# The last stage of an attention and two-MLP kernel: products of the result placed between the products of a and b

## The chip, the cores and the metric

The kernel runs on one core of a Trainium2 chip. Times are device microseconds of one execution; the kernel before takes 856.04 us as a median of 3 runs (854.52 to 856.62), lower is better. TensorE is called PE here, VectorE DVE, ScalarE ACT, GpSimd POOL, and SyncE, which issues DMAs, SP.

## The reference

Attention (a pooled one and a banded one, added) makes x of 2304 x 512. Two MLPs follow, and the change lies in the second:

```python
def _moe_ref(x, w_in, w_out):          # d_ff 2048
    h = x @ w_in
    g = h * np.cos(h)
    return (g @ w_out).astype(np.float32)

def _moe2_ref(x, w1, w2, w3, w_out):   # d_model 512, d_ff 1024
    a = x @ w1
    b = x @ w2
    h = a * b @ w3
    return (h @ w_out).astype(np.float32)
```

## The kernel before

The kernel is recorded by a small planner. Each piece of work is a generator (`Job`, lines 191 to 202) with an urgency; it asks for an engine, a buffer or a condition. `run` (264) gives an engine that its own cost estimates call free to the most urgent job whose inputs they call visible. The result is one fixed order of instructions for each engine; on the chip every engine takes its queue in that order and waits at the head of it for what is missing. All instructions are recorded in one helper, so all have line 131 in the profile, and one goes by tile names.

The second MLP is stage 2, the last 280 us. w3 @ w_out was multiplied beforehand into one matrix (`w5`), so the result is (a * b) @ w5. The 2304 tokens are taken in 3 blocks j of 768, d_ff in 8 slices f of 128, which makes 24 steps n = 8 j + f (`steps2`). In a step, PE makes 7 products `ps_ab` (128 x 384, `ab_job`, 993): a recombination scheme of Strassen's kind, in which 7 products of quarter matrices replace the 8 that a and b would need. Numbers are split into a high and a low part, so a product of PE is 3 matmuls for each half of the contraction, 6 in all (`mm3`, 401). `sums_job` (955) recombines the 7 products: ACT copies product 0 to SBUF, DVE then makes seven additions that read products 1 to 6, product 4 twice. These tiles are called `v`. Product 1 gives a0, half of a; the additions of product 5 and 6 complete b0 and a1. `m_half_job` (944) multiplies a and b for each half of the 768 tokens on POOL (`v<-v`), casts the high part on ACT (`m<-v`) and subtracts for the low part on POOL (`m<-v,m`). Six products `ps_o` (128 x 512, 3 matmuls each, `o_job`, 1020) then add the step's share of the result: o0 to o2 need half 0 of m, o3 to o5 half 1.

Two PSUM banks are left for `ps_ab`. They are used in turn, so product k + 2 waits until product k has been read by ACT or DVE. The other six banks hold `ps_o`, which accumulates over the 8 steps of a block; at the end of a block ACT and DVE copy the six tiles out (`o_out_job`, 1040).

`y_in_job` loads the next block's x as `yr` and makes the seven right-hand operands `y` of the 7 products: sums of quarters (`yr<-yr`, DVE) and, for each, a cast on ACT (`y<-yr`) and two subtractions on POOL or DVE (`y<-yr,y`). Buffers for these come free one by one while the last step of a block (n = 7 and n = 15) uses the old ones. `w5_back_job` splits a slice of w5 for each step (`w<-w5r` on ACT, `w<-w5r,w` on DVE).

Before the change the products of the result are a job of their own with urgency base + 1000.5, behind `ab_job` with base + 1000. PE takes an o product only when the planner holds that the next `ps_ab` can't start. Line 1001 keeps the two together: step n may begin when step n - 2 of the result is done.

Of the kernel before, what the change touches and what calls it, by code (L numbers as in the profile page):

```python
# [21 lines left out]
P = 128  # L22
# [5 lines left out]
F2 = DFF2 // P  # L28
# [14 lines left out]
N2 = 768  # L43
NH = N2 // 2
NCH2 = NT // N2
NQ = 7
# [12 lines left out]
OUT_BANKS = (4, 5, 6, 7, 2, 3)  # L59
# [11 lines left out]
def fused_kernel(ctx: ExitStack, tc: tile.TileContext, qk_block, v_block, qk_pool, v_pool,  # L71
# [63 lines left out]
    ve, se, pe, ge, sy = (Engine(*e) for e in (("ve", nc.vector), ("se", nc.scalar), ("pe", nc.tensor), ("ge", nc.gpsimd), ("sy", nc.sync)))  # L135
# [29 lines left out]
    done = {}  # L165
# [17 lines left out]
    def bank(n, name):  # L183

        return psum.tile([P, 512], F32, name=name, tag=f"bank{n}", bufs=1)
# [18 lines left out]
    def on(name, fn, *aps, when=lambda: True):  # L204
        yield name, fn, aps, when

    def until(cond):
        while not cond():
            yield "until", cond

    def at_hand(name):
        return sorted(x for x in free[name] if x[0] <= now[0])

    def take(name, n=1, spare=lambda: 0):

        yield from until(lambda: len(at_hand(name)) >= n + spare())
        got = at_hand(name)[:n]
        for x in got:
            free[name].remove(x)
        return got[0][1] if n == 1 else [x[1] for x in got]  # L220
# [15 lines left out]
    def give(name, slot, engine):  # L236
        free[name].append((ends[engine] + LATENCY[engine], slot))
# [5 lines left out]
    def count(key, n=1):  # L243
        done[key] = done.get(key, 0) + n
# [60 lines left out]
    w_t = {}  # L305
# [89 lines left out]
    def mm3(out_ap, st, mv, first, last):  # L395

        (sh, sl), (mh, ml) = st, mv
        pe.matmul(out_ap, lhsT=sh, rhs=ml, start=first, stop=False)
        pe.matmul(out_ap, lhsT=sl, rhs=mh, start=False, stop=False)
        pe.matmul(out_ap, lhsT=sh, rhs=mh, start=False, stop=last)  # L400
# [487 lines left out]
    ys, ms = {}, {}  # L888
    steps2 = [(j, f) for j in range(NCH2) for f in range(F2)]
# [45 lines left out]
    def value():  # L935
        yield from until(lambda: any(len(at_hand(name)) > keep for name, keep in VALUES))
        name = next(name for name, keep in VALUES if len(at_hand(name)) > keep)
        slot = yield from take(name)
        return buf(slot, "v", [NH]), slot

    def give_value(slot, engine):
        give(slot[0], slot, engine)
# [12 lines left out]
    def sums_job(n, base, ps):  # L955

        def product(k):
            yield from until(lambda: k in ps)
            return ps[k]

        def plus(x, k, last=True):
            at, p = ps[k]
            z, slot = yield from value()
            yield from on("ve", lambda: ve.tensor_tensor(out=z, in0=x, in1=p, op=ALU.add), x, p)
            if last:
                give("bank", at, "ve")
            return z, slot

        at, p = yield from product(0)
        p1, p1_slot = yield from value()  # L970
        yield from on("se", lambda: se.copy(p1, p), p)
        give("bank", at, "se")
        yield from product(1)
        a0, a0_slot = yield from plus(p1, 1)
        yield from product(2)
        u, u_slot = yield from plus(p1, 2)
        give_value(p1_slot, "ve")
        yield from product(3)
        v, v_slot = yield from plus(u, 3)
        yield from product(4)  # L980
        w, w_slot = yield from plus(u, 4, False)
        give_value(u_slot, "ve")
        b1, b1_slot = yield from plus(v, 4)
        yield from product(5)
        b0, b0_slot = yield from plus(v, 5)
        give_value(v_slot, "ve")
        Job(base + n, m_half_job(n, 0, a0, b0, a0_slot, b0_slot))
        yield from product(6)
        a1, a1_slot = yield from plus(w, 6)
        give_value(w_slot, "ve")  # L990
        Job(base + n, m_half_job(n, 1, a1, b1, a1_slot, b1_slot))

    def ab_job(base):
        yield from until(reached("h", NSTEPS))
        got = []
        while not {2, 3} <= set(got):
            got.append((yield from take("bank")))
        for at in got:
            give("bank" if at < 2 else f"bank{at}", at if at < 2 else 0, "pe")
        for n, (j, f) in enumerate(steps2):  # L1000
            yield from until(lambda: j in ys and done.get("o", 0) >= n - 1)
            ps = {}
            Job(base + n - 0.5, sums_job(n, base, ps))
            for k in range(NQ):
                q = NQ * f + k
                yield from until(lambda: k in ys[j] and ("w12", q // 2) in w_t)
                at = yield from take("bank")
                p = bank(at, "ps_ab")[:, :NH]
                w, (y, y_slot) = w_t["w12", q // 2][0][:, q % 2], ys[j][k]
                yield from on("pe", lambda: [mm3(p, (w[:, 0, c * P:(c + 1) * P], w[:, 1, c * P:(c + 1) * P]), (y[:, 0, c], y[:, 1, c]), c == 0, c == 1) for c in range(2)], y, w)  # L1010
                ps[k] = at, p
                if f == F2 - 1:
                    give("x", y_slot, "pe")
                if j == NCH2 - 1 and (q % 2 or q == NQ * F2 - 1):
                    give("w", w_t["w12", q // 2][1], "pe")
            if f == 0 and j + 1 < NCH2:
                Job(base + n + 4, y_in_job(j + 1))
            count("ab")

    def o_job(base):  # L1020
        for n, (j, f) in enumerate(steps2):
            if f == 0:
                ps = []
            for t in range(N2 // P):
                half, to = divmod(t, NH // P)
                yield from until(lambda: (n, half) in ms and ("w5", n) in w_t)
                (m, m_slot), (w, w_slot) = ms[n, half], w_t["w5", n]
                if f == 0:
                    yield from take(f"bank{OUT_BANKS[t]}")
                    ps.append(bank(OUT_BANKS[t], f"ps_o{t}"))  # L1030
                ts = slice(to * P, (to + 1) * P)
                yield from on("pe", lambda: mm3(ps[t], (m[:, 0, ts], m[:, 1, ts]), (w[:, 0, :], w[:, 1, :]), f == 0, f == F2 - 1), m, w)
                if f == F2 - 1:
                    Job(base + n - 2, o_out_job(j, t, ps[t]))
                if to == NH // P - 1:
                    give("g", m_slot, "pe")
            give("w", w_slot, "pe")
            count("o")

    def o_out_job(j, t, ps):  # L1040
        slot, name = (yield from take("t")), "ve" if t % 2 else "se"
# [15 lines left out]
    with tc.manual_schedule():  # L1057
# [76 lines left out]
        base = W5 + NSTEPS  # L1134
# [3 lines left out]
            Job(base + n - 6, w5_back_job(n))  # L1138
        Job(base - 8, y_in_job(0))
        Job(base + 1000, ab_job(base))  # L1140
        Job(base + 1000.5, o_job(base))
        run(reached("out", NT // P))


# [51 lines left out]
```

## Time and profile before

| | us |
|---|---|
| median of 3 runs | 856.04 (854.52 to 856.62) |
| profiled execution, device time | 858.45 |
| its span, first to last instruction | 856.7 |
| first `ps_ab` of stage 2 starts at | 575.04 |
| `ps_ab` in all, busy | 184.8 |
| `ps_o` in all, busy | 107.1 |

The profiled execution took 858.45 us, 2.4 us more than the median; its span is 856.7 us, and 1.75 us lie around it. In the timeline a row is a run of equal instructions: its start, how long it lasted, how many, and in brackets the time its engine stood idle before it and what ended that. Matmuls overlap, so a run's length contains about 0.16 us that the next run has begun in; starts are compared with starts. The chain of waits lists what led to the end, piece by piece, without such overlap.

### The profile page before, as it was taken

Reading aid. Unit: us, or ns where it says so; the run is one execution under the profiler, and the core shown is the slowest. Engines: PE = TensorE matmul, PEld = TensorE weight load, DVE = VectorE, ACT = ScalarE, POOL = GpSimd, SP = SyncE. Lnnn points to the kernel's source line nnn. Section 1 sums busy time; section 2 is a strip of 40 time slices with the busy share of each in tenths; the row PEclk is TensorE's granted clock in tenths of the full one; section 3 lists DMA queues with packets and bytes.
Section 4 is the critical chain, followed back from the end, with each engine's and each line's share of the span. In section 5 each row is a group of like instructions: output and inputs, shape, how many; then the busy total and the mean of one; then the engine's idle time right before and its main releaser. Section 6 shows DMA issues by size and latency. Waiting matters only on the chain.

```text
span 856.7 us, 14977 instructions
## 1 busy us (share of the span) xinstructions
PE 839.6 (98%) x5645; PEld 758.4 (89%) x5645; DVE 502.9 (59%) x897; ACT 446.6 (52%) x911; POOL 366.2 (43%) x330
## 2 busy tenths in 40 slices
PE   8999989999999999999999999999999999999998
PEld 7554579999999899998999999999999999999997
DVE  6988859975538783687446534625335633363442
ACT  2646689885767675677765756641112311241112
POOL 1013569855442345254533533524334633363322
PEclk9999999999999999999999999999999999999999
DMA  9989991131445532554255249681000500021011
GB/s 265 299 236 316 280 366 66 54 121 50 144 157 166 172 114 94 195 163 141 90 173 151 89 126 376 222 272 61 25 26 26 173 25 25 13 92 32 25 26 74
DMA packets 59625, 118.25 MB, mean 138 GB/s; under 512 B 18249, under 2 KB 25673, under 8 KB 59553
## 3 DMA queue, kind: packets, MB, share of 16 engines
q1 hardware_dynamic: 53040, 108.63, 39.7%
q10 hardware_dynamic: 6512, 8.67, 2.8%
q8 instruction: 44, 0.72, 0.4%
q14 instruction: 29, 0.23, 0.1%
HBM read 89.49 MB, written 27.79 MB: 137 GB/s over the span
## 4 chain that ended last, share of the span: by engine, by line
PE 83%; DVE 6%; DMA 5%; ACT 2%; issue 1%; ACTq 0%; POOL 0%; SPq 0%; DVEq 0%
PE ps_y L131 20%; PE ps_ab L131 20%; PE ps_h L131 19%; PE ps_o L131 12%; PE ps_w L131 5%; DVE t L131 2%; PE ps_av L131 2%; PE ps_tb L131 2%; DMA raw<-w3t 2%; DVE c L131 1%; PE ps_s L131 1%; DMA w_sc<-w 1%; PE ps_p L131 1%; DMA raw<-w_in 1%; PE ps_sb L131 1%
## 5 line engine op out<-in xcount | busy, mean ns | idle before, releaser
L131 PE MATMUL ps_y<-g,wo 128*128 128x384 f32 x1152 | 223.4, 338 | 0.4 <-POOL g L131 0.4
L131 PE MATMUL ps_h<-xs,wi 128*128 128x384 f32 x1152 | 219.5, 337 | 0.7 <-ACT ptp L131 0.5
L131 PEld LDWEIGHTS ps_y<-g,wo 128*128 128x128 f32 x1152 | 199.2, 188 | 4.6 <-issue 2.3
L131 PEld LDWEIGHTS ps_h<-xs,wi 128*128 128x128 f32 x1152 | 199.9, 188 | 3.5 <-issue 1.5
L131 PE MATMUL ps_ab<-y,w 128*128 128x384 f32 x1008 | 184.8, 336 | 0.9 <-DVE v L131 0.8
L131 PEld LDWEIGHTS ps_ab<-y,w 128*128 128x128 f32 x1008 | 176.8, 188 | 6.4 <-issue 1.4
L131 POOL TENSOR_TENSOR g<-c,g 128x384 fp32r<-128x384 f32 x96 | 106.5, 1109 | 157.1 <-ACT g L131 137.7
L131 DVE TENSOR_TENSOR v<-v,ps_ab 128x384 f32<-128x384 f32 x168 | 90.9, 553 | 139.8 <-ACT w L131 76.8
L131 ACT ACTIVATE c<-c 128x384 f32<-128x384 f32 x192 | 100.5, 524 | 36.2 <-DVE c L131 32.9
L131 POOL TENSOR_TENSOR v<-v 128x384 f32<-128x384 f32 x48 | 50.4, 1053 | 144.3 <-DVE v L131 142.5
L131 PE MATMUL ps_o<-w,m 128*128 128x512 f32 x432 | 107.1, 392 | 0.0
L131 DVE SCALAR_TENSOR_TENSOR c<-turns,ps_h 128x384 f32<-128x384 int32 x96 | 52.7, 549 | 79.2 <-ACT turns L131 71.5
L131 ACT CAST m<-v 128x384 fp32r<-128x384 f32 x48 | 24.5, 515 | 141.5 <-POOL v L131 141.5
L131 PEld LDWEIGHTS ps_o<-w,m 128*128 128x128 f32 x432 | 80.4, 188 | 14.1
L131 DVE SCALAR_TENSOR_TENSOR c<-c,ps_h 128x384 f32<-128x384 f32 x96 | 52.7, 549 | 55.8 <-ACT c L131 55.6
L131 ACT CAST g<-c 128x384 fp32r<-128x384 f32 x96 | 49.2, 512 | 41.5 <-DVE c L131 37.0
L131 ACT ACTIVATE turns<-ps_h 128x384 int32<-128x384 f32 x96 | 46.7, 487 | 37.2 <-PE ps_h L131 37.0
L131 PE MATMUL ps_w<-w,w 128*128 128x512 f32 x128 | 61.6, 608 | 1.5 <-DVE w L131 1.5
L131 ACT ACTIVATE t<-raw 128x512 f32<-128x512 f32 x72 | 47.8, 675 | 14.7 <-DMA raw<-w3t 5.9
L131 DVE TENSOR_SCALAR t<-t 128x512 int32<-128x512 int32 x72 | 46.7, 662 | 11.2 <-ACT t L131 11.2
L131 POOL TENSOR_TENSOR xs<-xb,xs 128x512 fp32r<-128x512 f32 (+1 forms) x24 | 27.1, 1129 | 51.0 <-ACT xs L131 47.3
L131 POOL TENSOR_TENSOR m<-v,m 128x384 fp32r<-128x384 f32 x48 | 47.8, 1017 | 0.0
(87 smaller groups left out, 862.5 us busy)
## 6 DMA issues: line engine op xcount, KB each, us to landing
w_sc<-w SPq DMA_DIRECT2D x56, 256.0 KB
w<-w_sc SPq DMA_DIRECT2D x28, 512.0 KB
raw<-w SPq DMA_DIRECT2D x24, 512.0 KB
raw<-w3t SPq DMA_DIRECT2D x16, 512.0 KB
raw<-w_in SPq DMA_DIRECT2D x16, 512.0 KB
raw<-w_out SPq DMA_DIRECT2D x16, 512.0 KB
w5r<-w_sc SPq DMA_DIRECT2D x24, 256.0 KB
kb<-qk_block SPq DMA_DIRECT2D x12, 408.0 KB
```

The lines of the kernel that those rows point to most:

```text
L131: return call(*args, **kw)
```

## The change

`o_job` is gone. `ab_job` itself issues the six products of the result of step n - 1 between the seven products of step n: one after product 2, 3, 4 and 5, two after product 6. A last round issues those of step 23 alone. The condition that step n - 2 of the result is done at the start of step n goes with it; the order now says it.

```diff
--- before.py
+++ after.py
@@ -997,45 +997,50 @@
             got.append((yield from take("bank")))
         for at in got:
             give("bank" if at < 2 else f"bank{at}", at if at < 2 else 0, "pe")
-        for n, (j, f) in enumerate(steps2):
-            yield from until(lambda: j in ys and done.get("o", 0) >= n - 1)
-            ps = {}
-            Job(base + n - 0.5, sums_job(n, base, ps))
+        ps_o = {}
+        for n in range(len(steps2) + 1):
+            if n < len(steps2):
+                j, f = steps2[n]
+                yield from until(lambda: j in ys)
+                ps = {}
+                Job(base + n - 0.5, sums_job(n, base, ps))
             for k in range(NQ):
-                q = NQ * f + k
-                yield from until(lambda: k in ys[j] and ("w12", q // 2) in w_t)
-                at = yield from take("bank")
-                p = bank(at, "ps_ab")[:, :NH]
-                w, (y, y_slot) = w_t["w12", q // 2][0][:, q % 2], ys[j][k]
-                yield from on("pe", lambda: [mm3(p, (w[:, 0, c * P:(c + 1) * P], w[:, 1, c * P:(c + 1) * P]), (y[:, 0, c], y[:, 1, c]), c == 0, c == 1) for c in range(2)], y, w)
-                ps[k] = at, p
-                if f == F2 - 1:
-                    give("x", y_slot, "pe")
-                if j == NCH2 - 1 and (q % 2 or q == NQ * F2 - 1):
-                    give("w", w_t["w12", q // 2][1], "pe")
-            if f == 0 and j + 1 < NCH2:
+                if n < len(steps2):
+                    q = NQ * f + k
+                    yield from until(lambda: k in ys[j] and ("w12", q // 2) in w_t)
+                    at = yield from take("bank")
+                    p = bank(at, "ps_ab")[:, :NH]
+                    w, (y, y_slot) = w_t["w12", q // 2][0][:, q % 2], ys[j][k]
+                    yield from on("pe", lambda: [mm3(p, (w[:, 0, c * P:(c + 1) * P], w[:, 1, c * P:(c + 1) * P]), (y[:, 0, c], y[:, 1, c]), c == 0, c == 1) for c in range(2)], y, w)
+                    ps[k] = at, p
+                    if f == F2 - 1:
+                        give("x", y_slot, "pe")
+                    if j == NCH2 - 1 and (q % 2 or q == NQ * F2 - 1):
+                        give("w", w_t["w12", q // 2][1], "pe")
+                if n:
+
+                    for t in {2: (0,), 3: (1,), 4: (2,), 5: (3,), 6: (4, 5)}.get(k, ()):
+                        yield from o_product(base, n - 1, t, ps_o)
+            if n < len(steps2) and f == 0 and j + 1 < NCH2:
                 Job(base + n + 4, y_in_job(j + 1))
-            count("ab")
-
-    def o_job(base):
-        for n, (j, f) in enumerate(steps2):
-            if f == 0:
-                ps = []
-            for t in range(N2 // P):
-                half, to = divmod(t, NH // P)
-                yield from until(lambda: (n, half) in ms and ("w5", n) in w_t)
-                (m, m_slot), (w, w_slot) = ms[n, half], w_t["w5", n]
-                if f == 0:
-                    yield from take(f"bank{OUT_BANKS[t]}")
-                    ps.append(bank(OUT_BANKS[t], f"ps_o{t}"))
-                ts = slice(to * P, (to + 1) * P)
-                yield from on("pe", lambda: mm3(ps[t], (m[:, 0, ts], m[:, 1, ts]), (w[:, 0, :], w[:, 1, :]), f == 0, f == F2 - 1), m, w)
-                if f == F2 - 1:
-                    Job(base + n - 2, o_out_job(j, t, ps[t]))
-                if to == NH // P - 1:
-                    give("g", m_slot, "pe")
-            give("w", w_slot, "pe")
-            count("o")
+            if n:
+                give("w", w_t["w5", n - 1][1], "pe")
+                count("o")
+
+    def o_product(base, n, t, ps):
+
+        (j, f), (half, to) = steps2[n], divmod(t, NH // P)
+        yield from until(lambda: (n, half) in ms and ("w5", n) in w_t)
+        (m, m_slot), (w, w_slot) = ms[n, half], w_t["w5", n]
+        if f == 0:
+            yield from take(f"bank{OUT_BANKS[t]}")
+            ps[t] = bank(OUT_BANKS[t], f"ps_o{t}")
+        ts = slice(to * P, (to + 1) * P)
+        yield from on("pe", lambda: mm3(ps[t], (m[:, 0, ts], m[:, 1, ts]), (w[:, 0, :], w[:, 1, :]), f == 0, f == F2 - 1), m, w)
+        if f == F2 - 1:
+            Job(base + n - 2, o_out_job(j, t, ps[t]))
+        if to == NH // P - 1:
+            give("g", m_slot, "pe")
 
     def o_out_job(j, t, ps):
         slot, name = (yield from take("t")), "ve" if t % 2 else "se"
@@ -1138,7 +1143,6 @@
             Job(base + n - 6, w5_back_job(n))
         Job(base - 8, y_in_job(0))
         Job(base + 1000, ab_job(base))
-        Job(base + 1000.5, o_job(base))
         run(reached("out", NT // P))
```

PE, the third step of stage 2, from its product 2 on; `y_...` are operands of a and b, `w_...` weights, `ps_o_...` the six banks of the result. Before:

```order
L131 MATMUL ps_ab<-y_6357,w_6236 128x384 x6
L131 MATMUL ps_ab<-y_6316,w_6236 128x384 x6
L131 MATMUL ps_ab<-y_6393,w_6259 128x384 x6
L131 MATMUL ps_ab<-y_6416,w_6259 128x384 x6
L131 MATMUL ps_o_6813<-w_6422,m 128x512 x3
L131 MATMUL ps_ab<-y_6643,w_6282 128x384 x6
L131 MATMUL ps_o_6859<-w_6422,m 128x512 x3
L131 MATMUL ps_o_6871<-w_6422,m 128x512 x3
L131 MATMUL ps_o_6878<-w_6422,m 128x512 x3
L131 MATMUL ps_o_6885<-w_6422,m 128x512 x3
L131 MATMUL ps_o_6892<-w_6422,m 128x512 x3
```

The same step on PE after the change:

```order
L131 MATMUL ps_ab<-y_6357,w_6236 128x384 x6
L131 MATMUL ps_o_6820<-w_6422,m 128x512 x3
L131 MATMUL ps_ab<-y_6316,w_6236 128x384 x6
L131 MATMUL ps_o_6835<-w_6422,m 128x512 x3
L131 MATMUL ps_ab<-y_6393,w_6259 128x384 x6
L131 MATMUL ps_o_6850<-w_6422,m 128x512 x3
L131 MATMUL ps_ab<-y_6416,w_6259 128x384 x6
L131 MATMUL ps_o_6864<-w_6422,m 128x512 x3
L131 MATMUL ps_ab<-y_6643,w_6282 128x384 x6
L131 MATMUL ps_o_6880<-w_6422,m 128x512 x3
L131 MATMUL ps_o_6888<-w_6422,m 128x512 x3
```

The work is the same; the two kinds alternate in five stretches each in place of two.

DVE, the last step of the first block (n = 7), from the last additions of step 6 on; `y_7397` and `y_7407` are operands 1 and 3 of the next block, `w_7381` is w5 of step 7, `yr` the quarters being subtracted. Before:

```order
L131 TENSOR_TENSOR v<-v,ps_ab 128x384 x5
L131 TENSOR_TENSOR y_7397<-yr,y_7397 128x384 x2
L131 TENSOR_TENSOR v<-v,ps_ab 128x384
L131 TENSOR_TENSOR y_7407<-yr,y_7407 128x384
L131 TENSOR_TENSOR w_7381<-w5r,w_7381 128x512
L131 TENSOR_TENSOR y_7407<-yr,y_7407 128x384
L131 TENSOR_TENSOR yr<-yr 128x2x384
L131 TENSOR_TENSOR v<-v,ps_ab 128x384
L131 TENSOR_TENSOR yr<-yr 128x2x384
```

The same place on DVE after the change, with the same tiles under other numbers (7396, 7411 and 7377):

```order
L131 TENSOR_TENSOR v<-v,ps_ab 128x384 x5
L131 TENSOR_TENSOR y_7396<-yr,y_7396 128x384 x2
L131 TENSOR_TENSOR w_7377<-w5r,w_7377 128x512
L131 TENSOR_TENSOR y_7411<-yr,y_7411 128x384 x2
L131 TENSOR_TENSOR yr<-yr 128x2x384
L131 TENSOR_TENSOR v<-v,ps_ab 128x384
L131 TENSOR_TENSOR yr<-yr 128x2x384
```

The addition of product 1 of step 7 (a0, the first single `v<-v,ps_ab` in either list) has moved behind four more operations: w, both halves of operand 3, and the first of the two large subtractions. The last step of the second block (n = 15) changes in the same way.

PE at the end of the program, from product 5 of step 23 on. Before:

```order
L131 MATMUL ps_ab<-y_8316,w_6683 128x384 x6
L131 MATMUL ps_o_8437<-w_8931,m 128x512 x3
L131 MATMUL ps_ab<-y_8339,w_6683 128x384 x6
L131 MATMUL ps_o_8496<-w_8931,m 128x512 x3
L131 MATMUL ps_o_8522<-w_8931,m 128x512 x3
L131 MATMUL ps_o_8527<-w_8931,m 128x512 x3
L131 MATMUL ps_o_8533<-w_8931,m 128x512 x3
L131 MATMUL ps_o_8540<-w_8931,m 128x512 x3
L131 MATMUL ps_o_8437<-w_9027,m 128x512 x3
```

After the change, from the same product:

```order
L131 MATMUL ps_ab<-y_8294,w_6683 128x384 x6
L131 MATMUL ps_o_8514<-w_8927,m 128x512 x3
L131 MATMUL ps_ab<-y_8312,w_6683 128x384 x6
L131 MATMUL ps_o_8527<-w_8927,m 128x512 x3
L131 MATMUL ps_o_8534<-w_8927,m 128x512 x3
L131 MATMUL ps_o_8470<-w_9023,m 128x512 x3
```

Between the last product of a and b and the first product of the last step's result stand two products of the result in place of five; the last row of each list is that first product (`w_9027`, `w_9023` are w5 of step 23).

## Rows read from the trace of the kernel before

**Rows 1.** The page's first part: busy time, share of the span, instructions.
```profile
PE 839.6 (98%) x5645; PEld 758.4 (89%) x5645; DVE 502.9 (59%) x897; ACT 446.6 (52%) x911; POOL 366.2 (43%) x330
```

**Rows 2.** Chain of waits, a regular step (start us, us, what; x counts matmuls).
```profile
640.26 6.27 PE ps_ab L131 x36
646.53 0.70 PE ps_o L131 x3
647.23 1.06 PE ps_ab L131 x6
648.29 3.44 PE ps_o L131 x15
```

**Rows 3.** Timeline of PE at the two changes of block.
```profile
651.57 2.27 PE L131 MATMUL ps_ab<-y,w 128*128 128x384 f32 x12
...
662.04 5.40 PE L131 MATMUL ps_ab<-y,w 128*128 128x384 f32 x30
667.86 2.34 PE L131 MATMUL ps_ab<-y,w 128*128 128x384 f32 x12 [0.41 <-DVE v L131]
670.04 0.86 PE L131 MATMUL ps_o<-w,m 128*128 128x512 f32 x3
...
760.41 2.35 PE L131 MATMUL ps_ab<-y,w 128*128 128x384 f32 x12 [0.41 <-DVE v L131]
```

**Rows 4.** Timeline of ACT in step 7, which starts at 651.57.
```profile
652.84 0.84 ACT L131 CAST y<-yr 128x768 fp32r<-128x768 f32 x1 [2.31 <-PE ps_ab L131]
653.58 0.47 ACT L131 COPY v<-ps_ab 128x384 f32<-128x384 f32 x1
...
654.68 0.62 ACT L131 CAST w<-w5r 128x512 fp32r<-128x512 f32 x1
```

**Rows 5.** Timeline of DVE in step 7 and just behind it.
```profile
653.71 1.03 DVE L131 TENSOR_TENSOR y<-yr,y 128x384 fp32r<-128x384 f32 x2 [4.82 <-ACT y L131]
654.65 0.55 DVE L131 TENSOR_TENSOR v<-v,ps_ab 128x384 f32<-128x384 f32 x1
...
655.58 0.69 DVE L131 TENSOR_TENSOR w<-w5r,w 128x512 fp32r<-128x512 f32 x1
...
656.77 0.96 DVE L131 TENSOR_TENSOR yr<-yr 128x768 f32<-128x768 f32 x1
657.65 0.55 DVE L131 TENSOR_TENSOR v<-v,ps_ab 128x384 f32<-128x384 f32 x1
...
663.77 1.84 DVE L131 TENSOR_TENSOR y<-yr,y 128x384 fp32r<-128x384 f32 x2
...
666.15 1.09 DVE L131 TENSOR_TENSOR w<-w5r,w 128x512 fp32r<-128x512 f32 x1
```

**Rows 6.** Timeline of PE and POOL at the end of the program.
```profile
843.00 0.86 PE L131 MATMUL ps_o<-w,m 128*128 128x512 f32 x3
...
844.76 7.68 PE L131 MATMUL ps_o<-w,m 128*128 128x512 f32 x33
...
846.56 1.99 POOL L131 TENSOR_TENSOR m<-v,m 128x384 fp32r<-128x384 f32 x2
```

**Rows 7.** Timeline of PE early in the program: its three longest waits.
```profile
15.38 1.71 PE L131 MATMUL ps_s<-qkd 64*72 64x144 f32 x8 [2.31 <-DVE qkd L131]
24.18 1.99 PE L131 MATMUL ps_w<-w,w 128*128 128x512 f32 x4 [1.55 <-DVE w L131]
115.78 0.71 PE L131 MATMUL ps_p<-ptp,vd 72*64 72x144 f32 x8 [1.77 <-DVE vd L131]
```

**Rows 8.** PE busy in stretches (bounds, length, busy, granted clock, DMA share, GB/s).
```profile
16.00:18.00 2.00, 2.00 (x10) 0.50 1.00 394
18.00:20.00 2.00, 2.00 (x14) 0.71 1.05 317
24.00:26.00 2.00, 1.82 (x4) 1.00 0.98 357
116.00:118.00 2.00, 2.00 (x17) 1.00 0.96 216
```

## The prediction

> **What bounds the kernel now.** I read the page's busy shares first: PE is busy 98% of the span and no other engine over 59% [rows 1]. So only what PE waits for, or does more slowly, can move the end. Next came the chain of waits over stage 2: from the first `ps_ab` to the last `ps_o` it is almost all PE, and in a regular step it shows four pieces without a gap [rows 2]. The timeline of PE then shows where PE does wait in this stage: once at each change of block, for an addition on DVE that frees a bank of `ps_ab` [rows 3]. Last, the timelines of ACT, DVE and POOL around the first of these places and around the end tell when the inputs come [rows 4 to 6].
>
> A model of PE's stage follows from rows 2. Six products of a and b in a row take 6.27, a single one 1.06: each further one costs (6.27 - 1.06) / 5 = 1.042, and an edge, where PE turns to them from the result, 1.06 - 1.042 = 0.018. Five products of the result take 3.44, one 0.70: each further one (3.44 - 0.70) / 4 = 0.685, and the edge 0.015. A pair of edges is 0.033, with the rounding of the rows 0.02 to 0.045. A regular step is 7 x 1.042 + 6 x 0.685 + 2 pairs = 11.47, as the four rows sum to.
>
> **Part 1, the finer alternation.** In each of 23 steps there are now 5 stretches of each kind, 115 pairs of edges in all; before there were 48 (two a step, one more at each change of block). 67 more pairs x 0.033 = +2.2. Bounds by rounding 1.3 to 3.0, and 0 if an edge is nothing but the profile's rounding.
>
> **Part 2, regular steps: no new wait.** Let R be the start of what stands behind product 5. At the end of the program R = 843.00, and the low part of half 0 is ready after the first of two subtractions, 846.56 + 1.99 / 2 = 847.55, that is R + 4.55; half 1 at R + 5.55 [rows 6]. The order of POOL and ACT in a regular step stays, and product 6 still stands one result product behind product 5, so these offsets hold. PE now comes to o0 after o3, product 6, o4 and o5, and products 0 to 2 of the next step: 0.70 + 1.06 + 1.385 + 3.15 = R + 6.3. That leaves 1.7 of slack; o3 comes 5.3 later still and needs half 1 only. If this cover were gone, each of 23 steps would pay what is missing. In the first step no result products stand between, so PE comes to o0 after only four products, 4.2 behind R, up to 0.4 early: +0.2 (0 to 0.4).
>
> **Part 3, the two changes of block: a long new wait.** Here the queue of DVE decides. In step 7 (start 651.57) product 3 needs the bank of product 1, which the addition a0 frees. Before, a0 ran at 654.65, right behind the two subtractions of operand 1 [rows 5]. Now w5's subtraction, both of operand 3 and the first large subtraction stand ahead of it. Walked through with these rows' durations:
> - ACT casts operand 1 at 652.84 and copies product 0 from 653.58 to 654.05 [rows 4]. Product 2 needs that bank; by the model PE is there at 651.57 + 2 x 1.042 + 0.018 = 653.67, and starts at 654.15. (0.1 from an engine's end to PE's start is an estimate; from the cast's end at 653.68 to DVE at 653.71 rows 4 and 5 show 0.03.) Before, a result product stood between and hid this.
> - DVE: operand 1 from 653.71 to 654.74; w, whose cast now comes before that of operand 3, to 655.34; operand 3, with its cast done at about 655.3, two subtractions of 0.5, to 656.38; the large subtraction, 0.96, to about 657.3; a0, 0.55, to 657.85 [rows 4, 5].
> - Product 3 can start at 657.95. Unhindered it would start at 651.57 + 3.15 + 0.70 = 655.42. Lost 2.53, and 0.08 for starting again: after the wait in rows 3 two products took 670.04 - 667.86 = 2.18 in place of 2.10. 2.6 in all.
>
> What is behind it: the additions of products 2 and 3 and the second large subtraction, which are done before PE needs their banks; the operands' casts and POOL's subtractions move later by as much as PE does. In step 8 PE's fixed order finds every bank free by the same walk. The same order stands at n = 15, so 2 x 2.6 = +5.2. Bounds from the nearest rows: nothing at all, if a0's place does not count; and if POOL works at the same time, the two pairs of operand subtractions cost 1.84 each in place of 1.03 and w 1.09 in place of 0.69 [rows 5], 2.0 more a change, +9.2. I take the uncontended rows, since POOL's last work on step 6, half 1, ends near 651.57 - 3.15 + 5.55 = 654.0.
>
> On this the Trainium skill (SBUF — State Buffer, Who interferes with whom) says that a DVE instruction with two SBUF inputs and a GpSimd instruction that reads SBUF can't share the port, and the loser blocks. Rows 5 agree (1.84 against 1.03); by that rule alone the sum would lie between +7.6 and +11.6, by when POOL works.
>
> The waits of before at the same places go. From 662.04 to 670.04 PE did seven products, 7 x 1.042 + 0.018 = 7.31, in 8.00 [rows 3]: 0.69 each, -1.4 together. What is late next there is part 3's own wait, a step earlier.
>
> **Part 4, the end.** Before, five products of the result covered the making of m of the last step, and 33 matmuls ran through from 844.76 [rows 6]. Now PE comes to the last step's o0 at R + 0.70 + 1.06 + 1.385 = R + 3.15, and half 0 is ready at R + 4.55: +1.4 (1.0, as the first of o0's three matmuls needs only the high part, to 1.7). Half 1 is there before o3, R + 5.55 against R + 6.6. The copies and DMAs behind are unchanged.
>
> **Sum.** 2.2 + 0.2 + 5.2 - 1.4 + 1.4 = +7.6. On the profiled execution's 858.45 (span 856.7 and 1.75 around it) that makes 866.05; that execution lies 2.4 above the median of the runs, so for a median 856.04 + 7.6 = **863.6**.
>
> **Rivals.**
> - *The clock falls in the new waits.* Early in the program a wait of 2.31 was followed by a granted clock of 0.50 (1.2 GHz) for 2 us and 0.71 for 2 more, while after waits of 1.55 and 1.77 it stayed at 1.00 (2.4 GHz) [rows 7, 8]. The new wait, 2.0 behind one of 0.5, lies between these. Price by rows 8: 2 x 0.50 + 2 x 0.29 = 1.6, twice, +3.2: 866.8. Against it: two of those three waits cost nothing. The Trainium skill (Perfetto Trace Analysis, Matmul Optimizations) also holds that matmuls should run back to back because the engine's power follows its use; rows 8 agree for one wait of three.
> - *Edges cost nothing*, and part 1's rounding is all: 856.04 + 5.4 = 861.4. The Trainium skill (TensorE: Matmul & The Clock Gate, Back-to-back issue gap) gives a spacing by the columns alone, N / 2.4 + 2.5 ns, which knows no edges. Rows 2 speak against it: 174 ns and 228 ns a matmul, not 162 and 216, and a single product costs more than its share in both kinds.
> - *Not slower: a0 is not late.* One place decides, the bank of product 1 in steps 7 and 15. If a0 starts by 655.42 - 0.1 - 0.55 = 654.8, as at 654.65 before, product 3 doesn't wait, and product 2's 0.5 is lost elsewhere in slack. Then +7.6 - 5.2 = +2.4, 858.4, no difference that can be measured. For it: DVE is busy 59% of the span only [rows 1]. Against it: DVE's queue is in order, and operand 3's cast can't be done before 655.
> - *Faster*: no edges, no wait at the changes, the end hidden: only the -1.4 stays, 854.6. Three terms would have to fail at once.
>
> **How the numbers follow.** A measurement of this kernel can tell about 0.3%, 2.6 us: faster is below 853.5, slower above 858.6. Chances: the forecast 0.60, the clock 0.15, free edges 0.10, a0 not late 0.08, faster or nothing 0.03, and 0.04 for contention that reaches part 3's upper bound (867.6). The forecast's own range is 861.5 to 865.5. For 8 in 10 I go down to 859.0, which leaves out a0 in time and the faster case, and up to 867.0, which takes in the clock and leaves out the contended bound. Slower: 0.60 + 0.15 + 0.10 + 0.04 and a quarter of the a0 case, 0.91. Within: the rest of that and most of the last rival, 0.07. Faster: 0.02.
>
> **What would show it.** Regular steps of 11.57 in place of 11.47, with ten pieces in the chain of waits and no idle time. In steps 7 and 15 a wait of PE of about 0.4 before product 2, for ACT, and of about 2.0 before product 3, for DVE, with a0 starting near 657.3 + 0.5 (the shift of the edges before it). No wait of 0.41 in steps 8 and 16. About 1.2 to 1.4 of idle PE before the last step's o0, for POOL. I am wrong if regular steps show waits for m, if a0 runs before operand 3, or if the granted clock leaves 1.00.

## The result and the profile after

The changed kernel takes 863.51 us, median of 4 runs (861.73 to 866.49); the kernel before, run beside it, 855.28. The ratio is 1.0101, with a 95% interval of 1.0066 to 1.0135: slower by 8.2 us. The forecast was 863.6, slower by 7.6.

The profiled execution of the changed kernel has a span of 859.9. The front of the program, which the change doesn't touch, ran 4.1 us shorter in it than in the profiled execution of before: the first `ps_ab` starts at 570.95, before at 575.04. So I compare what lies behind it, from the first `ps_ab` to the end of the span, and call it stage 2: 856.7 - 575.04 = 281.66 before, 859.9 - 570.95 = 288.95 after, +7.29. PE's share on the page is 98% as in [rows 1], and says nothing of this.

The chain of waits shows a regular step of the changed kernel, against [rows 2] (start us, us, what):

```profile
625.27 3.12 PE ps_ab L131 x18
628.39 0.70 PE ps_o L131 x3
629.09 1.06 PE ps_ab L131 x6
...
636.82 3.12 PE ps_ab L131 x18
```

Ten pieces without a gap, 636.82 - 625.27 = 11.55 a step; before it was 11.47 to 11.49. So 0.07 to 0.08 a step, and no new wait.

The timeline of PE in step 7, the first change of block, and the same place in step 15, against [rows 3] (start us, us, engine, line, operation, output and inputs, count, idle time before and what ended it):

```profile
648.21 2.25 PE L131 MATMUL ps_ab<-y,w 128*128 128x384 f32 x12
650.72 1.34 PE L131 MATMUL ps_ab<-y,w 128*128 128x384 f32 x6 [0.26 <-ACT v L131]
...
654.61 1.33 PE L131 MATMUL ps_ab<-y,w 128*128 128x384 f32 x6 [1.85 <-DVE v L131]
...
662.43 3.29 PE L131 MATMUL ps_ab<-y,w 128*128 128x384 f32 x18
...
749.76 1.31 PE L131 MATMUL ps_ab<-y,w 128*128 128x384 f32 x6 [1.85 <-DVE v L131]
```

Step 7 takes 662.43 - 648.21 = 14.22, and 2.67 more than a regular one; step 15 the same. Product 2 waits for ACT, product 3 for DVE. Before, both places ran through, and a wait of 0.41 came a step later; that one is gone. The idle time in brackets is less than what a wait costs: 0.26 + 1.85 = 2.11 are named, 2.67 are lost. A run's length reaches 0.16 into the next, so each wait is named 0.16 too short (and a very short one not at all), and the product behind it takes 1.33 or 1.34 in place of 1.22. So whole steps are compared below, from start to start. DVE's timeline in step 7, against [rows 5]:

```profile
650.33 1.24 DVE L131 TENSOR_TENSOR y<-yr,y 128x384 fp32r<-128x384 f32 x2 [2.75 <-ACT y L131]
651.49 0.68 DVE L131 TENSOR_TENSOR w<-w5r,w 128x512 fp32r<-128x512 f32 x1
652.09 1.01 DVE L131 TENSOR_TENSOR y<-yr,y 128x384 fp32r<-128x384 f32 x2
653.13 0.96 DVE L131 TENSOR_TENSOR yr<-yr 128x768 f32<-128x768 f32 x1
654.01 0.55 DVE L131 TENSOR_TENSOR v<-v,ps_ab 128x384 f32<-128x384 f32 x1
```

The addition a0 is the last of these lines, behind w5, operand 3 and the large subtraction, 5.80 behind the step's start. Product 3 starts as soon as a0 is done.

The end, timeline of PE and POOL, against [rows 6]:

```profile
848.61 1.78 PE L131 MATMUL ps_o<-w,m 128*128 128x512 f32 x7
...
850.48 1.97 POOL L131 TENSOR_TENSOR m<-v,m 128x384 fp32r<-128x384 f32 x2
...
851.53 4.15 PE L131 MATMUL ps_o<-w,m 128*128 128x512 f32 x17 [1.14 <-POOL m L131]
```

PE stands in the middle of the last step's o0 until the first of POOL's two subtractions is done. At the pace of [rows 6], 7.68 for 33, the 24 matmuls from 848.61 would be done at 854.20; they end at 851.53 + 4.15 = 855.68, 1.5 late.

### The profile page after: what moved, and what is told of

Same layout as the page of the kernel before. It is cut to its first block, busy times and chain, and to the rows that moved or that the text cites. A ratio compares the mean times of both kernels' runs of the same rounds, so it can differ in the third digit from the quotient of the medians.

```text
span 859.9 us, 14969 instructions
## 1 busy us (share of the span) xinstructions
PE 842.4 (98%) x5645; PEld 759.0 (88%) x5645; DVE 507.2 (59%) x897; ACT 446.2 (52%) x911; POOL 365.3 (42%) x330
## 4 chain that ended last, share of the span: by engine, by line
PE 85%; DVE 6%; DMA 4%; ACT 2%; issue 1%; SPq 0%; POOL 0%; ACTq 0%; DVEq 0%; POOLq 0%
PE ps_y L131 21%; PE ps_h L131 20%; PE ps_ab L131 19%; PE ps_o L131 11%; PE ps_w L131 6%; DVE t L131 2%; PE ps_av L131 2%; PE ps_tb L131 2%; DVE c L131 1%; DMA raw<-w_in 1%; PE ps_p L131 1%; PE ps_sb L131 1%; PE ps_s L131 1%; PE ps_t L131 1%; DMA vr<-v_pool 1%
## 5 line engine op out<-in xcount | busy, mean ns | idle before, releaser
L131 PE MATMUL ps_ab<-y,w 128*128 128x384 f32 x1008 | 196.7, 337 | 4.3 <-DVE v L131 3.7
L131 PEld LDWEIGHTS ps_ab<-y,w 128*128 128x128 f32 x1008 | 179.0, 188 | 17.0 <-DVE v L131 5.2
L131 PE MATMUL ps_o<-w,m 128*128 128x512 f32 x432 | 119.1, 394 | 1.1 <-POOL m L131 1.1
```

What stands on the lines that cost most here:

```text
L131: return call(*args, **kw)
```

## The experiments

Theory A is the prediction's account: DVE's queue, in which a0 is late, the edges, and the end. B says that a wait that is taken away only moves to the next place. C and D come up on the way. All runs stand in this table; "idle" is what PE's timeline names in stage 2, without the first step's and the end's. Stage 2 is that of one execution each. It holds 3.7 to 4.6 us of copies and DMAs behind PE's last matmul, and its first step, in which no product of the result stands, took 7.65 to 8.23; so a difference of some tenths between two rows need not be the edit's.

| kernel | median us (runs) | ratio to before, 95% | stage 2 | idle of PE |
|---|---|---|---|---|
| before | 855.28 (4) | | 281.66 | 2 x 0.41 |
| changed | 863.51 (4) | 1.0101 (1.0066 to 1.0135) | 288.95 | 2 x (0.26 + 1.85) |
| old tail | 861.04 (1) | | 287.16 | as changed |
| more edges | 866.44 (1) | | 293.1 | 2 x (0.26 + 2.08), 0.43 |
| inside products | 869.25 (1) | | 294.33 | 2 x (0.26 + 2.57), 0.52 |
| o0 early | 882.13 (1) | | 308.9 | 2 x (0.38 + 3.04), 0.47, 0.39, 1.58 |
| operands later | 869.92 (4) | 1.0166 (1.0148 to 1.0184) | 297.0 | 2 x (0.28 + 3.22), 0.30 |
| old places | 861.63 (4) | 1.0078 (1.0060 to 1.0096) | 287.53 | 2 x (0.26 + 1.69), 1.10 |
| old places at the changes | 866.08 (4) | 1.0132 (1.0109 to 1.0154) | 295.06 | 2 x (0.26 + 2.57) |
| cover back | 859.29 (4) | 1.0055 (1.0040 to 1.0071) | 285.23 | 2 x 0.34 |
| cover, old places | 854.94 (11) | 1.0004 (0.9995 to 1.0013) | 281.96 | 1.10 |
| cover, three steps | 854.22 (12) | 0.9985 (0.9976 to 0.9993) | 280.84 | none |
| one pair | 870.50 (4) | 1.0176 (1.0139 to 1.0212) | 296.8 | 0.2 a step, 1.92, 1.98 |

**The end alone.** The last step goes back to the old places.

```diff
-for t in {2: (0,), 3: (1,), 4: (2,), 5: (3,), 6: (4, 5)}.get(k, ()):
+for t in ({5: (0,), 6: (1, 2, 3, 4, 5)} if n == len(steps2) - 1 else {2: (0,), 3: (1,), 4: (2,), 5: (3,), 6: (4, 5)}).get(k, ()):
```

> The changed kernel, with the result's products of step 22 placed as before the change (one behind product 5, five behind product 6 of step 23), all else as changed. Theory A (two products in place of five no longer cover the making of m at the end): the 1.14 of idle PE before the last step's o0 goes and stage 2 falls from 288.95 by 1.4 to 287.5. Rival (the end is set by the copies and DMAs of the result, or the wait only moves to o3): stage 2 within 0.3 of 288.95.

Its timeline of PE at the end runs through, as in [rows 6]:

```profile
847.36 7.68 PE L131 MATMUL ps_o<-w,m 128*128 128x512 f32 x33
```

Stage 2 is 1.79 shorter than the changed kernel's. Of that 0.27 lies in the first step, which this edit doesn't touch: the first 60 matmuls show 10.96 here and 11.23 there. The other 1.52 is the end's price, as in the profile.

**The edges.** o's first matmul is put between the halves of products 2 to 6, ten pairs a step in place of five.

```diff
+for c in range(2):
...
+    if n and k >= 2 and c == 0:
+        yield from o_product(base, n - 1, k - 2, ps_o, 1)
```

> The changed kernel, with five of the six result products of a step split: their first matmul stands between the two halves of products 2 to 6, the other two behind the product. 10 pairs of edges in a regular step in place of 5, the same matmuls. Theory A (each turn of PE from one kind to the other costs, 0.027 a pair by 11.55 against 11.47): a regular step of 11.55 + 5 x 0.027 = 11.68, stage 2 longer by about 3. Rival (spacing by columns alone; the longer step comes from something else): 11.55 as it is.

Timeline of PE, a regular step of this run:

```profile
628.25 0.39 PE L131 MATMUL ps_o<-w,m 128*128 128x512 f32 x1
628.48 0.69 PE L131 MATMUL ps_ab<-y,w 128*128 128x384 f32 x3
629.01 0.63 PE L131 MATMUL ps_o<-w,m 128*128 128x512 f32 x2
629.47 0.70 PE L131 MATMUL ps_ab<-y,w 128*128 128x384 f32 x3
630.01 0.39 PE L131 MATMUL ps_o<-w,m 128*128 128x512 f32 x1
```

From 628.25 to 630.01 it is 1.76 for nine matmuls, as in the changed kernel from a single o to the next (0.70 + 1.06), with twice the edges. The step took 11.58, 0.03 over the changed kernel's. So the price of 0.033 for every edge pair fails: three more pairs cost 0.07 to 0.08 and the next five 0.03. This run's stage 2 is longer mostly for other reasons: its wait of 2.08 in step 7 was followed by a fall of the clock (last section), and step 10 has a wait of 0.43.

The next run keeps five pairs and puts o0 to o3 between the halves of products 3 to 6.

```diff
+        if n and c == 0 and 3 <= k <= 6:
+            yield from o_product(base, n - 1, k - 3, ps_o)
...
+for t in ({6: (4, 5)} if n < len(steps2) else {0: (0, 1, 2, 3, 4, 5)}).get(k, ()):
```

> The same five pairs of changes of kind in a step as in the changed kernel, but o0 to o3 stand between the two halves of products 3 to 6 in place of between two products. If the 0.08 us of a regular step is the price of the change of kind wherever it stands: 11.55 us a step. If it is the price of a product that begins behind another kind (a change inside a product cost 0.005 in the run with ten pairs): 11.48 to 11.50. The waits at the changes of block stay (0.26 and 1.85, theory A), and the wait at the end is shorter or the same, 0.9 to 1.4.

A regular step took 11.56 (in the chain of waits from 627.16 to 638.72), so where the five stand doesn't matter. The traces, read matmul by matmul, show why ten pairs cost hardly more than five. In a stretch of five result products the first nine matmuls start 0.224 to 0.236 apart and the later ones 0.227; products of a and b settle at 0.173 in a long stretch, but a single one has three gaps of 0.177 to 0.185. The slow places begin with the second matmul of a stretch, so cutting a short stretch once more leaves some of them out. At the settled pace alone a step would take 42 x 0.173 + 18 x 0.227 = 11.35; over that are 0.13 with two pairs, 0.20 with five and 0.23 with ten. What makes these places slow stays open.

**The offsets.** o0 of the step before is put behind product 0.

```diff
-for t in {2: (0,), 3: (1,), 4: (2,), 5: (3,), 6: (4, 5)}.get(k, ()):
+for t in {0: (0,), 3: (1,), 4: (2,), 5: (3,), 6: (4, 5)}.get(k, ()):
```

> The changed kernel, with the first result product of a step moved from behind product 2 to behind product 0. By the offset R + 4.55 for the low part of half 0, PE comes to it at R + 4.2: theory A (the slack of a regular step is 1.7 and two products more are 2.1) gives a wait for POOL in every regular step, 0.1 to 0.45 each, stage 2 longer by 3 to 10. Rival (m is ready much earlier, and a regular step has more slack than that): no wait, stage 2 within 0.5 of 288.95.

The chain of waits, a regular step of this run:

```profile
627.83 1.01 POOL v L131
628.83 0.98 POOL m L131
...
629.86 0.74 PE ps_o L131 x2
```

The chain now runs over POOL's product and its subtraction to o0, and a step takes 11.94 to 11.96, 0.4 longer and within the range expected. PE came to o0 some 2.1 earlier and lost 0.4, which bears out the slack of 1.7 and the offset of 4.55 of part 2 for regular steps. The timeline names no idle time there, as the delay is too short for it. At the two changes PE waited 3.04 there: then POOL also has the operands' work, and there is no slack.

**DVE's queue.** The operands of the next block are asked for later, so that the additions come first in DVE's queue.

```diff
-                Job(base + n + 4, y_in_job(j + 1))
+                Job(base + n + 6.75, y_in_job(j + 1))
```

> The changed kernel, with the making of the next block's operands less urgent than the additions of steps 7 and 15, so that a0 stands earlier in DVE's queue and ACT copies product 0 before it casts operand 1. Theory A (DVE's queue order at the two changes of block makes the long waits): ACT's wait of 0.26 goes, DVE's wait of 1.85 before product 3 falls under 1.0; each of the two steps takes about 12.5 in place of 14.2, stage 2 (first a/b product to the end) falls from 288.95 by 3.4 to about 285.5. Rival B (there is simply too much for DVE and ACT at the change of block, whatever the order): the wait turns up at another product of step 7 or 8 and stage 2 stays within 0.7 of 288.95.

Step 7 became regular: 11.56, no wait. But step 8 got a longer one, for POOL. PE's timeline, then POOL's:

```profile
665.11 0.50 PE L131 MATMUL ps_o<-w,m 128*128 128x512 f32 x1 [0.28 <-ACT m L131]
668.83 1.22 PE L131 MATMUL ps_o<-w,m 128*128 128x512 f32 x2 [3.22 <-POOL m L131]
...
675.66 1.23 PE L131 MATMUL ps_ab<-y,w 128*128 128x384 f32 x6
```

```profile
658.29 5.25 POOL L131 TENSOR_TENSOR y<-yr,y 128x384 fp32r<-128x384 f32 x4 [5.83 <-ACT y L131]
663.50 2.42 POOL L131 TENSOR_TENSOR v<-v 128x384 f32<-128x384 f32 x2
...
667.79 1.95 POOL L131 TENSOR_TENSOR m<-v,m 128x384 fp32r<-128x384 f32 x2
```

The large subtractions come later in DVE's queue, so POOL gets its operands later, and the work on m stands behind them. The saving of 2.67 became a wait of 3.5 and a fall of the clock. Theory A's number fails and B's kind of answer comes, dearer: step 8 takes 18.3. That DVE's queue holds product 3 up is borne out; that relieving it gains anything is not.

**The old order.** Is it the order at all? The changed code with the old places everywhere. Theory C would be that one job for both kinds costs by itself.

```diff
-for t in {2: (0,), 3: (1,), 4: (2,), 5: (3,), 6: (4, 5)}.get(k, ()):
+for t in {5: (0,), 6: (1, 2, 3, 4, 5)}.get(k, ()):
```

> The changed kernel's single job, with the kernel before's places of the result's products in it (o0 behind product 5, o1 to o5 behind product 6). Theory A (the loss is the order in which TensorE takes the products): the second stage, first ps_ab to the end of the span, takes 281 to 282.5 us as in the kernel before (281.7), regular step 11.48, no wait at the end. Rival C (the loss comes from making one job of two, which ties the schedule of the other engines): 284 us or more, with waits that the kernel before doesn't have.

861.63, not 855. The regular steps were at 11.48 and the end ran through; steps 7 and 15 lost 2.9 each, as much as in the changed kernel or more, and step 10 had a wait of 1.10. PE in step 7, and DVE:

```profile
651.55 2.46 PE L131 MATMUL ps_ab<-y,w 128*128 128x384 f32 x12 [0.26 <-ACT v L131]
655.70 2.67 PE L131 MATMUL ps_ab<-y,w 128*128 128x384 f32 x12 [1.69 <-DVE v L131]
```

```profile
651.15 1.03 DVE L131 TENSOR_TENSOR y<-yr,y 128x384 fp32r<-128x384 f32 x2 [4.82 <-ACT y L131]
652.10 0.55 DVE L131 TENSOR_TENSOR v<-v,ps_ab 128x384 f32<-128x384 f32 x1
...
654.22 0.96 DVE L131 TENSOR_TENSOR yr<-yr 128x768 f32<-128x768 f32 x1
655.10 0.55 DVE L131 TENSOR_TENSOR v<-v,ps_ab 128x384 f32<-128x384 f32 x1
```

Here a0 stands where it stood before, right behind operand 1 (652.10), and product 3 doesn't wait. PE waits all the same, one product later, for the next addition, which now has w5, operand 3 and the large subtraction ahead of it. So a0's place alone isn't what decides. The kernel before had the same queue of DVE [rows 5] and no wait, and what it had besides shows in its PE timeline of step 7:

```profile
653.68 0.86 PE L131 MATMUL ps_o<-w,m 128*128 128x512 f32 x3
...
656.48 2.92 PE L131 MATMUL ps_o<-w,m 128*128 128x512 f32 x12
```

There its planner had put o0 in front of product 2 and o1 to o4 in front of product 4, 0.70 + 2.76 of result products while PE's banks were not free. A regular step has none there. That is theory D: what the fixed order takes away is the cover at the two changes, whatever the fixed order is.

The run beside it, old places in steps 7 and 15 alone, says the same with its sizes.

```diff
+for t in ({5: (0,), 6: (1, 2, 3, 4, 5)} if n in (7, 15) else {2: (0,), 3: (1,), 4: (2,), 5: (3,), 6: (4, 5)}).get(k, ()):
```

> The changed kernel with the old places in the two steps at a change of block (7 and 15) alone. Theory A: these two steps lose the 2 x 2.67 us of waits, and get back at most the old 2 x 0.69: second stage 283.6 to 285.0 us (changed kernel 288.95, before 281.66); what is left over before is the end (1.4) and the regular steps (some 1.5). Rival B (the wait only moves on to the first result product of steps 8 and 16, which stands early there): 287 us or more, with waits of 1 us or more for GpSimd's m in steps 8 and 16.

```profile
655.88 5.24 PE L131 MATMUL ps_ab<-y,w 128*128 128x384 f32 x18 [2.57 <-DVE v L131]
```

Both theories missed. The wait before product 3 grew from 1.85 to 2.57, by 0.72: one result product (0.70) less stands in front of it, and DVE's queue is that of the changed kernel, so a0 comes at the same time. The run with o0 inside product 3 shows the same 2.57. Stage 2 grew by 6.1, though: in both runs the clock fell behind these waits (last section).

**Cover back.** DVE's queue stays as in the changed kernel, a0 late; only in steps 7 and 15 the result products stand earlier.

```diff
+for t in ({1: (0, 1), 2: (2, 3), 3: (4,), 6: (5,)} if n in (7, 15) else {2: (0,), 3: (1,), 4: (2,), 5: (3,), 6: (4, 5)}).get(k, ()):
```

> The changed kernel with other places in the two steps at a change of block (7 and 15) alone: o0 and o1 behind product 1, o2 and o3 behind product 2, o4 behind product 3, o5 behind product 6. DVE's queue stays as in the changed kernel there, with a0 behind operand 1, w5, operand 3 and the first large subtraction. Theory D (the loss is the cover: the kernel before had result products in front of products 2 and 4 there; a0's late place costs nothing if 2.77 us of result products stand before product 3, against 0.70 + 1.85 needed): no waits in steps 7 and 15, some 0.3 to 1.0 in front of o0 of steps 8 and 16 for POOL's m; second stage 284.2 to 285.6 us (changed kernel 288.95). Theory A as predicted (a0's place in DVE's queue decides, whatever covers it): the waits stay, 287 us or more.

PE in step 7 (start 647.36), then DVE's a0:

```profile
649.45 1.55 PE L131 MATMUL ps_o<-w,m 128*128 128x512 f32 x6
...
651.88 1.55 PE L131 MATMUL ps_o<-w,m 128*128 128x512 f32 x6
653.77 1.31 PE L131 MATMUL ps_ab<-y,w 128*128 128x384 f32 x6 [0.34 <-DVE v L131]
...
659.81 3.32 PE L131 MATMUL ps_ab<-y,w 128*128 128x384 f32 x18
```

```profile
653.17 0.55 DVE L131 TENSOR_TENSOR v<-v,ps_ab 128x384 f32<-128x384 f32 x1
```

a0 starts 653.17 - 647.36 = 5.81 behind the step's start, in the changed kernel 5.80: as late as there. Product 3 waits 0.34 in place of 0.26 + 1.85, and stage 2 is 285.23, in the range that D expected (0.27 of the 3.72 saved lies in the first step). The step takes 659.81 - 647.36 = 12.45, 0.9 over a regular one in place of 2.67: the cover gives back two thirds, not all. I had the place of what remains wrong: o0 of steps 8 and 16 doesn't wait, but product 3 comes some 0.6 late all the same, and product 6 some 0.35. There products 4, 5 and 6 now stand in a row, and product 6 waits for the second addition that reads product 4, too short a wait for the timeline to name.

The same places at the two changes, and the old ones elsewhere:

```diff
+for t in ({1: (0, 1), 2: (2, 3), 3: (4,), 6: (5,)} if n in (7, 15) else {5: (0,), 6: (1, 2, 3, 4, 5)}).get(k, ()):
```

> The kernel before's places everywhere (o0 behind product 5, the others behind 6), but in the two steps at a change of block the places of the run e11: o0, o1 behind product 1, o2, o3 behind 2, o4 behind 3, o5 behind 6. Theory D: 2 x 2.9 us go against the run with the old places everywhere (second stage 287.5), and the 2 x 0.69 of the kernel before don't come back, as o0 of steps 8 and 16 stands behind product 5: second stage 280.3, or up to 281.5 if the wait of 1.10 in step 10 stays; ratio to the kernel before 0.997 to 1.000. Theory A: 285 or more.

Stage 2 is 281.96, 5.57 less than with the old places everywhere, and the timeline names no wait in steps 7, 8, 15 and 16. Steps 7 and 15 take 11.86, where a regular one takes 11.48: the short wait of product 6 is there here too. So C falls: with one job the kernel is as fast as before (1.0004). What remains is a wait of 1.10 in step 10. The timeline of all engines there:

```profile
682.20 1.99 POOL L131 TENSOR_TENSOR y<-yr,y 128x384 fp32r<-128x384 f32 x2
...
684.22 0.96 DVE L131 TENSOR_TENSOR yr<-yr 128x768 f32<-128x768 f32 x1 [5.02 <-ACT w L131]
...
685.70 1.01 DVE L131 TENSOR_TENSOR v<-v,ps_ab 128x384 f32<-128x384 f32 x2
...
686.30 3.42 PE L131 MATMUL ps_ab<-y,w 128*128 128x384 f32 x18 [1.10 <-DVE v L131]
```

DVE's large subtraction overwrites what POOL still reads: it starts at 684.22, as POOL ends at 682.20 + 1.99 = 684.19. ACT's `w`, which the line names, ends there too, but that is a tile of w5; by the code (`y_in_job`) POOL's two subtractions read the quarter that DVE overwrites. The additions stand behind it. This place can be covered as well:

```diff
-for t in ({1: (0, 1), 2: (2, 3), 3: (4,), 6: (5,)} if n in (7, 15) else {5: (0,), 6: (1, 2, 3, 4, 5)}).get(k, ()):
+for t in ({1: (0, 1), 2: (2, 3), 3: (4,), 6: (5,)} if n in (7, 15) else {2: (0, 1), 6: (2, 3, 4, 5)} if n == 10 else {5: (0,), 6: (1, 2, 3, 4, 5)}).get(k, ()):
```

> The run e12 with one more step's places changed: in step 10, where PE waited 1.10 us before product 3 for an addition that stands in DVE's queue behind a large subtraction, o0 and o1 stand behind product 2 (1.39 us of result products before product 3). DVE's queue stays. Theory D: that wait goes too, no wait is left from the first ps_ab to the end but the 0.2 to 0.3 of the first step; second stage 280.8 us (e12 281.96, before 281.66), ratio to the kernel before 0.998 to 1.000. Rival (a wait that is covered there comes back at the next addition or at POOL's m): 282 us or more.

```profile
684.30 3.31 PE L131 MATMUL ps_ab<-y,w 128*128 128x384 f32 x18
687.45 1.56 PE L131 MATMUL ps_o<-w,m 128*128 128x512 f32 x6
688.84 4.70 PE L131 MATMUL ps_ab<-y,w 128*128 128x384 f32 x24
...
696.14 6.44 PE L131 MATMUL ps_ab<-y,w 128*128 128x384 f32 x36
```

The wait of 1.10 is gone: step 10 takes 696.14 - 684.30 = 11.84, in the run before this one 12.87. It is still 0.36 over a regular step, in the short wait of product 6, and so are steps 7 and 15, by 0.4. Stage 2 is 280.84, and that this meets the 280.8 expected is in part luck: 0.24 of the 1.12 saved lies in the first step. The kernel takes 854.22 against 855.36 for the kernel before beside it, ratio 0.9985 (0.9976 to 0.9993), a small gain that the interval just tells from none. The kernel before lost 0.69 in each of steps 8 and 16; that is gone, and 0.35 to 0.4 in each of steps 7, 10 and 15 has come in. From the first `ps_ab` to the start of the last matmul this execution is 0.3 shorter than that of before. Whether the other 0.5 of stage 2, behind PE's last matmul, belongs to the change isn't shown. A result product between products 5 and 6 of these three steps wasn't tried.

**One lump.** All six behind product 5, and the operands later.

```diff
-for t in {2: (0,), 3: (1,), 4: (2,), 5: (3,), 6: (4, 5)}.get(k, ()):
+for t in ({5: (0,), 6: (1, 2, 3, 4, 5)} if n >= len(steps2) - 1 else {5: (0, 1, 2, 3, 4, 5)}).get(k, ()):
...
-                Job(base + n + 4, y_in_job(j + 1))
+                Job(base + n + 6.75, y_in_job(j + 1))
```

> All six result products of a step together behind product 5 (one pair of changes in a step, against two before and five after), old places in the last step, and the operands of the next block's products asked for later by 2.75 steps' worth of priority. If a pair costs 0.027: regular step 11.45 us; if the later operands also take away the waits of the block changes without new ones (the result products stand 3.2 us later than in the run where POOL's m came late by 3.2): second stage 279.5 to 281 us, against 281.66 before. Rival B (the wait moves on to POOL's m in steps 8 and 16): 0.3 to 1.5 us there at each, second stage 281 to 283.

A miss: 870.50. A regular step took 11.96, with an idle time of 0.23 before product 4. PE's timeline, and DVE's before it:

```profile
618.90 2.39 PE L131 MATMUL ps_ab<-y,w 128*128 128x384 f32 x12 [0.23 <-DVE v L131]
```

```profile
617.30 1.08 DVE L131 TENSOR_TENSOR w<-w5r,w 128x512 fp32r<-128x512 f32 x1
```

w5's subtraction stands among the additions and takes 1.08, against 0.69 in [rows 5], and in five products in a row nothing covers it. By the starts of the matmuls product 4 comes 0.39 late and takes 0.12 longer, which is the whole 0.5 over the 11.45 expected; the 0.23 that is named is a part of it.

## Why the prediction was right, and where not

- **Part 1, the edges: right in direction, too large, and wrong as a price per pair.** +2.2 forecast. Measured: 0.07 to 0.08 in each of the 21 steps that are neither of the two changes of block, +1.6, inside the bounds 1.3 to 3.0. But five more pairs a step cost 0.03, not 0.16: the 0.033 read from [rows 2] doesn't carry over to another number of pairs.
- **Part 2, regular steps: right, but for the first step.** No wait for m in any; o0 two products earlier shows a chain over POOL. The +0.2 was forecast for the o0 that stands in step 1. That step takes 11.55 like every other, so the term was nothing. The changed kernel's execution is 0.3 longer in the step ahead of it, 7.95 against 7.65, in which no product of the result stands; the run with the old tail, which has the same first step, took 7.68. So 0.3 in the sum below stands where the forecast has 0.2, and only by chance.
- **Part 3, the changes of block: size right, reason half right.** +2.6 each forecast, +2.67 measured, with the two waits at the products and for the engines named, a0 at 5.80 against the walk's 657.3 - 651.57 = 5.7, and the old -1.4 gone. The uncontended rows were the right choice: only operand 1 took longer, 1.24 in place of 1.03. The step that failed is "one place decides, the bank of product 1" and the rival built on it, that with a0 in time the 5.2 would be saved. In the two runs with a0 early (old places, and operands later) the time was lost again, before product 4 or in step 8; a0 just as late cost 0.9 a step in place of 2.67 under cover. [Rows 3] leave out the result products that the planner had moved within step 7. The prediction knew of the one in front of product 2, but not of the four in front of product 4, and did not ask why the same queue of DVE, with its late addition at 657.65 [rows 5], held nobody up before.
- **Part 4, the end: right.** +1.4 forecast, 1.5 measured in the profile and with the old tail.
- **The rival of the clock** stayed away in the changed kernel (1.00 throughout both waits). That was a near thing, as the last section shows: it came in six of the experiments, behind waits of about the same length too. Its price of 1.6 was too low: in the run with later operands the stretch from 668.83 to 675.66 holds 0.47 + 1.06 + 0.70 + 1.06 + 0.70 = 3.99 of work by the changed kernel's rows and took 6.83, 2.8 more.

The sum, 2 x 2.67 - 1.38 + 1.6 + 1.5 + 0.3 = 7.4, stands against 7.29 measured in stage 2 and 8.2 between the medians. Where the rest of the 8.2 lies is not shown, as one execution of each kernel has a trace; the first `ps_ab` started at 570.34 to 575.04 in the traces of all kernels, so the front of the program, which no edit touches, varies by more than that. That the median forecast, 863.6, and the one measured, 863.51, differ by 0.1 is luck: the four runs lie between 861.73 and 866.49.

## What to carry to other kernels

Where a planner has put work into a stretch in which another engine is late, a fixed order has to put work there too, and its regular pattern doesn't know that stretch: look in the trace of before at what stands differently at the irregular steps, not only at what waits there. When an addition is late, ask first how much independent work can stand in front of its reader; moving it forward in its own queue only made the next one late, or the engine behind it.

## What the runs showed of the hardware

Which waits of PE brought TensorE's clock from 2.4 to 1.2 GHz was not told by their length alone. It stayed at 1.00 after 1.69 and 1.85 in steps 7 and 15 of the old places and of the changed kernel and after 1.87 in the run with the old tail, and fell after 1.92 and 1.98 in the run with one lump. In the run with o0 early it fell after a wait of only 1.58, which had others of 0.47 and 0.39 just ahead of it. With ten pairs a step a wait of 2.08 was followed by a fall in step 7 and by none in step 15. After 2.57, 3.04 and 3.22 it fell each time. PE in stretches (bounds, length, busy, granted clock, DMA share, GB/s), first the run with ten pairs, behind its wait in step 7, then the run with later operands, in step 8:

```profile
655.00:657.00 2.00, 1.59 (x7) 0.81 0.07 22
657.00:659.00 2.00, 2.00 (x7) 0.50 0.00 0
```

```profile
669.00:671.00 2.00, 2.00 (x6) 0.50 0.00 0
...
673.00:675.00 2.00, 2.00 (x8) 0.51 0.06 25
```

Here a wait of 3.2 us cost 2.8 more in the clock. In the run with one lump the two products behind the wait of 1.92 took 3.46, behind one of 0.23 they took 2.39. So a wait behind which the clock falls is dearer than the timeline's idle time says; here that was so behind one of 1.58 and behind ones of 3.22.
